# Second layer of a spectral mixture kernel: its seven products a unit in two pairs of runs in place of four

## The chip, the cores and the metric

The kernel runs on one core of one Trainium2 chip. The metric is device time in microseconds, the median of the timed runs. Beside them one execution was recorded by the hardware profiler, and all rows come from it. TensorE (PE) runs the matrix products and its weight loads (PEld), VectorE (DVE) and ScalarE (ACT) the element-wise work, GpSimd (POOL) the scattered stores, SyncE (SP) the other transfers.

## The reference

```python
def _attn_ref(x, filt_r, filt_i):            # x: 8 x 3072 x 256
    Y = np.fft.rfft(x, axis=1) * (filt_r + 1j * filt_i)[None, :, :]
    return np.fft.irfft(Y, n=x.shape[1], axis=1)

def _moe_ref(x, w_gate, w_output_gate, w1, w2):   # one of 8 experts for each token, 256 -> 1024 -> 256
    ...
    h = np.maximum(x[mask] @ w1[e], 0.0)
    out[mask] = gate_w[mask, None] * eom[mask, e, None] * (h @ w2[e])

def _moe2_ref(x, w_in, w_out):               # 256 -> 2048 -> 256, the second layer
    h = np.maximum(x @ w_in, 0.0)
    return h * h @ w_out
```

The three follow one another on 24576 tokens. The change touches the last one alone.

## The kernel before, in words

The kernel works through the filter, the routing and the first (expert) layer, and then through the second layer, which takes a little over half of the span. All sums are made from split numbers: each float32 operand is the sum of a high part and a low part (`bh`, `bl` for tokens, `wsh`, `wsl` and `woh`, `wol` for weights, `hh`, `hl` for the hidden values), and each product is three matrix products into the same PSUM place: high by high, and the two mixed ones.

The second layer has 48 tiles of 512 tokens (t) and in each 8 units of 256 hidden columns (u), 384 units in all. A unit has an up part and a down part.

The up part, `up2`, makes a 2 x 2 block product from seven products in place of eight, on block sums that were made ahead (`split_t` for the tokens, `decode_all` for the weights). The helper `prod` issues one product, three matrix products of 128 x 128 weights with 256 columns. Products 0, 4, 5 and 2 add up in one PSUM bank, V; products 3 and 6 in another, G; product 1 stands in a third, P. The banks are handed over by copies: after product 0 ScalarE copies V to `s1` (L906), after product 3 it copies G to `p5` (L908), after product 4 V to `u2` (L913), after product 2 V to the result block `C[:, 2]` (L921). VectorE makes `C[:, 0]` from P and s1 (L911), `C[:, 3]` from V and p5 (L917), `C[:, 1]` from G and u2 (L918), and then q, the square of the rectified C (L923). V has two buffers, G and P have one each. Where a bank is written again after a copy, the matrix product's weight load waits for that copy.

`split_h` makes the high part `hh` of q on ScalarE (L930) and the low part `hl` on VectorE (L932). `down2` then issues 24 matrix products (m from 0 to 23) into the two output banks of the tile; after the last unit of a tile ScalarE copies the banks out (L951), and GpSimd scatters them to the output rows (L954).

All are Python generators: each `next` issues the instructions up to the next `yield`, and the order in which the loop in `steps_m` takes them is the order of the instructions on every engine. In step n the loop issues the up part of unit n, `split_h` of unit n - 1 and the down part of unit n - 2. Before the change it does so in four parts: 6 up and 3 down matrix products, 6 and 6, 6 and 9, 3 and 6. `hh` stands in the second part, `hl` in the third. Between units `split_t` issues one of its four steps for the next tile, in four of eight units. Below, a run is a row of matrix products of one kind (up or down), and a pair is a run of up and the run of down behind it.

Of the kernel before, what the change touches and what calls it, by code (L numbers as in the profile page):

```python
# [17 lines left out]
ALU = mybir.AluOpType  # L18
# [84 lines left out]
def spectral_moe_kernel(ctx: ExitStack, tc: tile.TileContext, x, filt_r, filt_i, w_gate, w_og, w1, w2,  # L103
                        w_in, w_out, c_ma, c_mi, c_mb, c_mb2, c_sg, c_cum, out):
    nc = tc.nc
# [608 lines left out]
    def py_tiles(t):  # L714
        return [pl["psY2" if t % 2 and "psY2" in pl else "psY"].tile([128, TT], F32, name=f"py{h}") for h in range(2)]
# [82 lines left out]
    def up(t, f):  # L798
        xh, xl = X[t]
        w = width[t]  # L800
        h1, l1 = (a[:, 0] for a in W[t, f // 2])
        f2 = f % 2
        ps = ph_tile()[:, 0:w]
        n = 0
        for c in range(2):
            for a, b in ((h1, xh), (h1, xl), (l1, xh)):
                nc.tensor.matmul(ps, a[:, c, f2 * 128:(f2 + 1) * 128], b[:, c, 0:w], start=n == 0, stop=n == 5)  # L807
                n += 1
        hh = pl["hp"].tile([128, TT], F32R, name="hh")[:, 0:w]
        hl = pl["hp"].tile([128, TT], F32R, name="hl")[:, 0:w]  # L810
        nc.scalar.activation(hh, ps, AF.Relu)  # L811
        tick[:] = [hh[0:1, 0:1].bitcast(F32)]
        nc.vector.scalar_tensor_tensor(hl, ps, 0.0, hh.bitcast(F32), op0=ALU.max, op1=ALU.subtract)  # L813
        H[t, f] = hh, hl
# [77 lines left out]
    def up2(t, u):  # L892

        bh, bl, _ = X2[t]
        wsh, wsl = w2nd[0:2]

        def prod(ps, a, b, start):
            for n, (x, y) in enumerate(((wsh, bh), (wsh, bl), (wsl, bh))):
                nc.tensor.matmul(ps, x[:, u, a], y[:, b], start=start and n == 0, stop=n == 2, skip_group_check=True)  # L899

        bank = lambda name: pl[name].tile([128, TT], F32, name="px" if name == "psX" else "ph")[:, 0:256]
        V, G, P = bank("psH"), bank("psX"), bank("psH2")
        s1, p5, u2 = (pl["sp"].tile([128, 256], F32, name=n) for n in ("s1", "p5", "u2"))
        C = pl["cp"].tile([128, 4, 256], F32, name="C")
        prod(V, 0, 0, True)
        nc.scalar.copy(s1, V)  # L906
        prod(G, 3, 3, True)
        nc.scalar.copy(p5, G)  # L908
        yield
        prod(P, 1, 1, True)  # L910
        nc.vector.tensor_tensor(C[:, 0], P, s1, ALU.add)  # L911
        prod(V, 4, 4, False)
        nc.scalar.copy(u2, V)  # L913
        yield
        prod(G, 6, 2, False)
        prod(V, 5, 5, False)
        nc.vector.tensor_tensor(C[:, 3], V, p5, ALU.add)  # L917
        nc.vector.tensor_tensor(C[:, 1], G, u2, ALU.add)  # L918
        yield
        prod(V, 2, 6, False)  # L920
        nc.scalar.copy(C[:, 2], V)  # L921
        q = pl["cp"].tile([128, 4, 256], F32, name="q")
        nc.vector.scalar_tensor_tensor(q, C, 0.0, C, op0=ALU.max, op1=ALU.mult)  # L923
        H2[t, u] = q
        yield

    def split_h(t, u):
        q = H2[t, u]
        hh, hl = (pl["h2p"].tile([128, 4, 256], F32R, name=n) for n in ("hh2", "hl2"))
        nc.scalar.copy(hh, q)  # L930
        yield
        nc.vector.tensor_tensor(hl, q, hh.bitcast(F32), ALU.subtract)  # L932
        H2[t, u] = hh, hl
        yield

    def down2(t, u):

        hh, hl = H2[t, u]
        woh, wol = w2nd[2:4]
        if u == 0:  # L940
            Z[t] = [p.rearrange("p (c d) -> p c d", c=2) for p in py_tiles(t)]
        for m in range(24):
            k, i, c, n = m // 12, m // 6 % 2, m // 3 % 2, m % 3
            x, w = ((hh, woh), (hl, woh), (hh, wol))[n]
            nc.tensor.matmul(Z[t][k][:, c, :], x[:, 2 * i + k, c * 128:(c + 1) * 128], w[:, 2 * u + i, :],  # L945
                             start=u == 0 and m in (0, 12), stop=u == NU - 1 and m in (11, 23), skip_group_check=True)
            if u == NU - 1 and m in (11, 23):
                if k == 0:
                    Z[t].append(pl["oup"].tile([128, 4, D], F32, name="ou"))
                ou = Z[t][2]  # L950
                nc.scalar.copy(ou[:, 2 * k:2 * k + 2, :], Z[t][k])  # L951
                io = X2[t][2]
                for c in range(2 * k, 2 * k + 2):
                    nc.gpsimd.indirect_dma_start(out=outv[4 * t + c], out_offset=bass.IndirectOffsetOnAxis(ap=io[:, c:c + 1], axis=0),  # L954
                                                 in_=ou[:, c, :], in_offset=None)
            if m in (2, 8, 17):
                yield
        del H2[t, u]
        if u == NU - 1:
            del X2[t], Z[t]  # L960
        yield
# [3 lines left out]
    units2 = [(t, u) for t in range(NTILE2) for u in range(NU)]  # L965
# [3 lines left out]
    def step_1(t, f):  # L969

        last = t + 1 == KP
        if f == 5 and t + 2 == KP:
            start_t(KP)
        if f == 1 and t + 1 >= KP:
            for n in (t + 2, t + 3) if last else (t + 3,):
                if n < NMAIN:
                    start_t(n)
        if f == 1 and last:
            gather(KP)
        if f == 3 and t + 2 < NMAIN and t + 2 != KP:  # L980
            gather(t + 2)
        if f % 2 == 1:

            g = NQ * t + f // 2 + 2
            if NQ * KP <= g < NQ * NMAIN:
                split_w(*divmod(g, NQ))
            if NQ * KP <= g + 2 < NQ * NMAIN:
                load_w(*divmod(g + 2, NQ))
        if t + 1 < NMAIN:
            at = (4, 5, 7) if last else (2, 4, 6)  # L990
            if f == at[0]:
                scale_x(t + 1)
            if f == at[0] + 1:
                put_ids(t + 1)
            if f in at[1:]:
                turn_x(t + 1, at.index(f) - 1)
        elif f == 1:
            load_t(0)
            load_t(1)
        if f not in (1, 5) and dec and next(dec[0], 0) == 0:  # L1000
            dec.clear()
            dcs.close()
            pl["bp0"] = ctx.enter_context(tc.tile_pool(name="bp0", bufs=1))
            pl["bp0"].tile([128, 16], F32, name="pad0")
        if t + 1 == NMAIN and f >= 3:
            if f == 3:
                first.append(split_t(0))
            next(first[0], None)

    def extra(t):  # L1010

        start_t(t)
        gather(t)
        for q in range(3):
            load_w(t, q)
        scale_x(t)
        put_ids(t)
        turn_x(t, 0)
        turn_x(t, 1)
        for f in range(NF + 1):  # L1020
            if f < NF:
                if f % 2 == 0:
                    split_w(t, f // 2)
                    if f == 0:
                        load_w(t, 3)
                up(t, f)
            if f:
                down(t, f - 1)

    def steps_m():  # L1030
        for n in range(len(jobs) + LAG1):
            if n < len(jobs):
                t, f = jobs[n]
                up(t, f)
                step_1(t, f)
            if n >= LAG1:
                down(*jobs[n - LAG1])
            yield
        used = nc.values_load(usedi[0:1, 0:1], min_val=0, max_val=NTILE_T)
        with tc.If(used > NTILE_T - NX):  # L1040
            for t in range(NMAIN, NTILE1):
                extra(t)
        m1.close()
        xgs.close()
        open_m2()
        st = iter(())
        for n in range(len(units2) + 2):
            g = up2(*units2[n]) if n < len(units2) else iter(())
            t, u = units2[min(n, len(units2) - 1)]
            d = down2(*units2[n - 2]) if n >= 2 else iter(())  # L1050
            for part in range(4):
                next(g, None)
                if part == 0 and 0 < n <= len(units2):
                    sh = split_h(*units2[n - 1])
                if part in (1, 2) and n:
                    next(sh, None)
                next(d, None)
            if u == 2 and t + 2 < NTILE2:
                load_t(t + 2)
            if u == 3 and t + 1 < NTILE2:  # L1060
                st = split_t(t + 1)
            next(st, None)
            yield
# [41 lines left out]
    gens = {"a": steps_a(), "b": steps_b(), "c": steps_c()}  # L1105
    done = {"a": 0, "b": 0, "c": 0}
    m = steps_m()
    dec = []
    pre = None
    ready_m = False  # L1110
    close_at = len(order) - 1 - order[::-1].index("b") + 2
    for i, k in enumerate(order):
# [3 lines left out]
        n = done["a"]  # L1116
# [62 lines left out]
```

## Time and profile before

| what | value |
|---|---|
| timed runs, median (lowest to highest) | 3820.49 us (3819.74 to 3821.23) |
| the profiled execution, its own time | 3807.87 us |
| its span | 3806.2 us |
| TensorE busy | 3757.5 us, 99% of the span |
| VectorE busy | 2769.3 us, 73% |
| ScalarE busy | 1980.2 us, 52% |
| granted TensorE clock, mean | 0.998 |

Matrix products overlap in the records: one lasts some 0.28 us, but the next starts after less than half of that. What counts is the time from start to start. The matrix products of the second layer stand at L899 (up) and L945 (down).

### The profile page before, as it was taken

The page shows a single profiled execution, that of the slowest core. Times are in us where ns is not written, and L with a number is a line of the kernel's source. Part 1 is how long each engine was busy: PE and PEld are TensorE (multiplying, and loading weights), DVE is VectorE, ACT ScalarE, POOL GpSimd, SP SyncE. Part 2 cuts the span into 40 slices and gives each one's busy share as a digit, 9 for nine tenths or more (in the row PEclk, how much of TensorE's full clock was granted, in tenths as well). Part 3 has the DMA queues.
Part 4 walks back from the last instruction along what each step waited for, and adds up shares of the span by engine and source line. Part 5 has one row for each costly group of instructions (what it writes and reads, how often), then busy time and mean ns, then how long its engine had stood idle before and what let it go on. Part 6 is the DMA issues. An engine that isn't in the chain of part 4 may idle for free.

```text
span 3806.2 us, 73317 instructions
## 1 busy us (share of the span) xinstructions
PE 3757.5 (99%) x27256; PEld 3510.1 (92%) x27256; DVE 2769.3 (73%) x5041; ACT 1980.2 (52%) x3912; POOL 608.2 (16%) x641
## 2 busy tenths in 40 slices
PE   8999999999999999999999999999999999999998
PEld 7888877888888888888999999999999999999998
DVE  6687685688888865665777777777777777777775
ACT  6476473454554554554555555555555555555554
POOL 3477575000000000000011001000100110011001
PEclk9999999999999999999999999999999999999999
DMA  6333322455555554553000100010000001000100
GB/s 192 100 114 117 107 90 100 153 168 160 172 174 165 173 165 151 162 157 93 23 26 26 29 23 29 23 29 23 29 25 27 24 29 29 24 26 26 29 18 18
DMA packets 262750, 309.29 MB, mean 81 GB/s; under 512 B 75154, under 2 KB 206195, under 8 KB 262387
## 3 DMA queue, kind: packets, MB, share of 16 engines
q1 hardware_dynamic: 242928, 252.39, 21.9%
q0 software_dynamic: 18432, 51.93, 3.8%
q8 instruction: 215, 3.52, 0.4%
q14 instruction: 149, 1.21, 0.1%
q10 hardware_dynamic: 1026, 0.23, 0.0%
HBM read 224.01 MB, written 80.45 MB: 80 GB/s over the span
## 4 chain that ended last, share of the span: by engine, by line
PE 52%; issue 1%; POOL 0%; POOLq 0%; DVE 0%; ACT 0%; DVEq 0%; ACTq 0%
PE py L945 27%; PE ph L899 18%; PE px L899 7%; POOL out_dram L954 0%; POOLq L1174 0%; DVE C L917 0%; ACT u L913 0%; DVEq L917 0%; POOLq L954 0%; ACTq L913 0%
## 5 line engine op out<-in xcount | busy, mean ns | idle before, releaser
L945 PE MATMUL py<-woh,hh 128*128 128x256 f32 x3072 | 857.1, 279 | 0.0
L945 PE MATMUL py<-woh,hl 128*128 128x256 f32 x3072 | 852.8, 278 | 0.5 <-DVE hl L932 0.5
L945 PE MATMUL py<-wol,hh 128*128 128x256 f32 x3072 | 852.9, 278 | 0.0
L954 POOL DMA_INDIRECT out_dram<-ou,ix x192 | 214.0, 1115 | 2924.3 <-ACT ou L951 2880.5
L945 PEld LDWEIGHTS py<-woh,hl 128*128 128x128 f32 x3072 | 579.9, 189 | 1.0 <-DVE hl L932 0.9
L945 PEld LDWEIGHTS py<-woh,hh 128*128 128x128 f32 x3072 | 579.9, 189 | 0.0
L945 PEld LDWEIGHTS py<-wol,hh 128*128 128x128 f32 x3072 | 576.3, 188 | 0.0
L811 ACT ACTIVATE hh<-ph 128x512 fp32r<-128x512 f32 (+1 forms) x472 | 252.2, 534 | 577.4 <-PE ph L807 560.6
L899 PE MATMUL ph<-bh,wsh 128*128 128x256 f32 x1920 | 540.8, 282 | 6.0 <-SPq L1040 4.8
L899 PE MATMUL ph<-bl,wsh 128*128 128x256 f32 x1920 | 537.1, 280 | 0.0
L899 PE MATMUL ph<-bh,wsl 128*128 128x256 f32 x1920 | 536.8, 280 | 0.0
L813 DVE SCALAR_TENSOR_TENSOR hl<-ph,hh 128x512 fp32r<-128x512 f32 (+1 forms) x472 | 286.5, 607 | 254.8 <-ACT hh L811 254.1
L923 DVE SCALAR_TENSOR_TENSOR q<-C 128x1024 f32<-128x1024 f32 x384 | 470.5, 1225 | 1.8 <-ACT C L921 1.8
L932 DVE TENSOR_TENSOR hl<-q,hh 128x1024 fp32r<-128x1024 f32 x384 | 466.8, 1216 | 1.1 <-ACT hh L930 1.1
L917 DVE TENSOR_TENSOR C<-ph,p 128x256 f32<-128x256 f32 x384 | 163.3, 425 | 412.7 <-ACT hh L930 403.1
L921 ACT COPY C<-ph 128x256 f32<-128x256 f32 x384 | 144.1, 375 | 525.2 <-PE ph L899 525.2
L930 ACT CAST hh<-q 128x1024 fp32r<-128x1024 f32 x384 | 403.5, 1051 | 1.3 <-DVE q L923 1.3
L899 PEld LDWEIGHTS ph<-bh,wsh 128*128 128x128 f32 x1920 | 362.4, 189 | 7.2 <-issue 4.9
L899 PEld LDWEIGHTS ph<-bh,wsl 128*128 128x128 f32 x1920 | 360.9, 188 | 0.0
L899 PEld LDWEIGHTS ph<-bl,wsh 128*128 128x128 f32 x1920 | 360.9, 188 | 0.0
L824 PE MATMUL py<-hh,wh 128*128 128x512 f32 (+1 forms) x944 | 341.0, 368 | 0.0
L807 PE MATMUL ph<-xh,wh 128*128 128x512 f32 (+1 forms) x944 | 339.3, 359 | 0.0
(265 smaller groups left out, 8086.7 us busy)
## 6 DMA issues: line engine op xcount, KB each, us to landing
r<-in_moe_w_dram SPq DMA_DIRECT2D x448, 256.0 KB
xt<-in_x_dram SPq DMA_DIRECT2D x48, 512.0 KB
r<-ytd SPq DMA_DIRECT2D x48, 512.0 KB
xg<-srt SPq DMA_DIRECT2D x41, 544.0 KB
ytd<-yt SPq DMA_DIRECT2D x41, 512.0 KB
xg<-srt SPq DMA_DIRECT2D x18, 272.0 KB
ytd<-yt SPq DMA_DIRECT2D x18, 256.0 KB
raw<-in_moe_w_in_dram SPq DMA_DIRECT2D x16, 256.0 KB
```

The costliest lines, as they stand in the source:

```text
L807: nc.tensor.matmul(ps, a[:, c, f2 * 128:(f2 + 1) * 128], b[:, c, 0:w], start=n == 0, stop=n == 5)
L811: nc.scalar.activation(hh, ps, AF.Relu)
L813: nc.vector.scalar_tensor_tensor(hl, ps, 0.0, hh.bitcast(F32), op0=ALU.max, op1=ALU.subtract)
L824: nc.tensor.matmul(Y[t][h], a[:, f % 2, h * 128:(h + 1) * 128], b, start=f == 0 and i == 0, stop=f == NF - 1 and i == 2, skip_group_check= ...
L899: nc.tensor.matmul(ps, x[:, u, a], y[:, b], start=start and n == 0, stop=n == 2, skip_group_check=True)
L917: nc.vector.tensor_tensor(C[:, 3], V, p5, ALU.add)
L921: nc.scalar.copy(C[:, 2], V)
L923: nc.vector.scalar_tensor_tensor(q, C, 0.0, C, op0=ALU.max, op1=ALU.mult)
L930: nc.scalar.copy(hh, q)
L932: nc.vector.tensor_tensor(hl, q, hh.bitcast(F32), ALU.subtract)
L945: nc.tensor.matmul(Z[t][k][:, c, :], x[:, 2 * i + k, c * 128:(c + 1) * 128], w[:, 2 * u + i, :], start=u == 0 and m in (0, 12), stop=u == ...
L954: nc.gpsimd.indirect_dma_start(out=outv[4 * t + c], out_offset=bass.IndirectOffsetOnAxis(ap=io[:, c:c + 1], axis=0), in_=ou[:, c, :], in_o ...
```

## The change

The seven products of a unit keep their operands, banks and copies. What changes is where the generators yield and in which order the loop takes them. Product 2 of a unit, with its copy and the square, is issued in the next step, behind product 0 of the next unit (`next(old, None)`). From the fourth step on, a step issues 18 up (product 0, product 2 of the unit before, products 3, 1, 4, 6), then `hh`, then 15 down, then `hl`, then 3 up (product 5), then 9 down. In the first step that has a down part (n = 2) the 18 and 15 are parted into 9 and 6 and again 9 and 9. The sum `C[:, 1]` is made ahead of `C[:, 3]`.

```diff
@@ up2
         prod(V, 0, 0, True)
         nc.scalar.copy(s1, V)
+        yield
         prod(G, 3, 3, True)
         nc.scalar.copy(p5, G)
         yield
@@ up2
         prod(V, 4, 4, False)
         nc.scalar.copy(u2, V)
-        yield
         prod(G, 6, 2, False)
+        nc.vector.tensor_tensor(C[:, 1], G, u2, ALU.add)
+        yield
         prod(V, 5, 5, False)
         nc.vector.tensor_tensor(C[:, 3], V, p5, ALU.add)
-        nc.vector.tensor_tensor(C[:, 1], G, u2, ALU.add)
         yield
@@ down2
-            if m in (2, 8, 17):
+            if m in (5, 14):
                 yield
@@ steps_m
+        none = iter(())
+        old = none
         for n in range(len(units2) + 2):
-            g = up2(*units2[n]) if n < len(units2) else iter(())
+            g = up2(*units2[n]) if n < len(units2) else none
             t, u = units2[min(n, len(units2) - 1)]
-            d = down2(*units2[n - 2]) if n >= 2 else iter(())
-            for part in range(4):
-                next(g, None)
-                if part == 0 and 0 < n <= len(units2):
-                    sh = split_h(*units2[n - 1])
-                if part in (1, 2) and n:
-                    next(sh, None)
+            d = down2(*units2[n - 2]) if n >= 2 else none
+            next(g, None)
+            next(old, None)
+            sh = split_h(*units2[n - 1]) if 0 < n <= len(units2) else none
+            next(g, None)
+            if n == 2:
                 next(d, None)
+            next(g, None)
+            next(sh, None)
+            if n > 2:
+                next(d, None)
+            next(d, None)
+            next(sh, None)
+            next(g, None)
+            next(d, None)
+            old = g
```

## Rows read from the trace of the kernel before

**Rows 1.** The page, engines: busy us (share of the span) xinstructions.

```profile
PE 3757.5 (99%) x27256; PEld 3510.1 (92%) x27256; DVE 2769.3 (73%) x5041; ACT 1980.2 (52%) x3912; POOL 608.2 (16%) x641
```

**Rows 2.** Windows: 500 us, then the four pairs of one unit; columns as headed.

```profile
core 0: us, PE busy (x) PEld busy (x) DVE busy (x) ACT busy (x) POOL busy (x), PEclk, DMA share, GB/s
2250.00:2750.00 500.00, 500.00 (x4290) 500.00 (x4290) 369.68 (x574) 260.26 (x547) 50.62 (x46) 1.00 0.09 26
...
2603.23:2604.30 1.07, 1.07 (x12) 1.07 (x11) 1.07 (x2) 1.07 (x3) 0.00 (x0) 1.00 0.72 172
2604.30:2605.67 1.37, 1.37 (x15) 1.37 (x13) 0.56 (x2) 0.80 (x4) 0.00 (x0) 1.00 0.00 0
2605.67:2607.44 1.77, 1.77 (x17) 1.77 (x16) 0.79 (x3) 0.89 (x1) 0.00 (x0) 1.00 0.00 0
2607.44:2608.47 1.03, 1.03 (x11) 1.03 (x10) 1.03 (x2) 0.38 (x1) 0.00 (x0) 1.00 0.00 0
```

**Rows 3.** Timeline of TensorE, same unit: start us, length us, engine, line, operation.

```profile
2604.65 0.28 PE L899 MATMUL ph<-bh,wsh 128*128 128x256 f32 x1
...
2605.67 0.28 PE L899 MATMUL px<-bh,wsh 128*128 128x256 f32 x1
...
2606.50 0.28 PE L945 MATMUL py<-woh,hl 128*128 128x256 f32 x1
...
2607.44 0.28 PE L899 MATMUL ph<-bh,wsh 128*128 128x256 f32 x1
```

**Rows 4.** Timeline, same unit: ScalarE's operations and G's last product of product 3.

```profile
2605.51 1.05 ACT L930 CAST hh<-q 128x1024 fp32r<-128x1024 f32 x1
...
2608.05 0.38 ACT L921 COPY C<-ph 128x256 f32<-128x256 f32 x1 [1.49 <-PE ph L899]
...
2609.07 0.28 PE L899 MATMUL px<-bh,wsl 128*128 128x256 f32 x1
...
2609.44 0.38 ACT L908 COPY p<-px 128x256 f32<-128x256 f32 x1
```

**Rows 5.** Timeline of VectorE, same unit.

```profile
2606.65 0.42 DVE L917 TENSOR_TENSOR C<-ph,p 128x256 f32<-128x256 f32 x1 [1.31 <-ACT hh L930]
...
2606.99 0.41 DVE L918 TENSOR_TENSOR C<-px,u 128x256 f32<-128x256 f32 x1
...
2607.32 1.22 DVE L932 TENSOR_TENSOR hl<-q,hh 128x1024 fp32r<-128x1024 f32 x1
...
2608.46 1.23 DVE L923 SCALAR_TENSOR_TENSOR q<-C 128x1024 f32<-128x1024 f32 x1
```

**Rows 6.** Timeline, the second unit, ahead of all down products (PEld: weight loads).

```profile
1780.77 0.28 PE L899 MATMUL ph<-bh,wsl 128*128 128x256 f32 x1
...
1781.08 0.38 ACT L906 COPY s<-ph 128x256 f32<-128x256 f32 x1
...
1781.45 0.28 PE L899 MATMUL ph<-bh,wsl 128*128 128x256 f32 x1
...
1781.51 0.19 PEld L899 LDWEIGHTS ph<-bh,wsh 128*128 128x128 f32 x1
...
1781.73 0.28 PE L899 MATMUL ph<-bl,wsh 128*128 128x256 f32 x1
...
1782.20 0.28 PE L899 MATMUL px<-bh,wsl 128*128 128x256 f32 x1
```

**Rows 7.** Timeline, a unit in which a weight load was held once.

```profile
3220.91 0.42 DVE L917 TENSOR_TENSOR C<-ph,p 128x256 f32<-128x256 f32 x1 [1.66 <-ACT hh L930]
...
3221.24 0.28 PE L945 MATMUL py<-wol,hh 128*128 128x256 f32 x1
...
3221.39 0.19 PEld L899 LDWEIGHTS ph<-bh,wsh 128*128 128x128 f32 x1
...
3221.62 0.29 PE L899 MATMUL ph<-bl,wsh 128*128 128x256 f32 x1
...
3221.97 0.28 PE L945 MATMUL py<-woh,hl 128*128 128x256 f32 x1
```

More of the change, by code (lines that the diff above doesn't have):

```diff
@@ L913, in up2 @@
         nc.scalar.copy(u2, V)
+        prod(G, 6, 2, False)
+        nc.vector.tensor_tensor(C[:, 1], G, u2, ALU.add)
         yield
-        prod(G, 6, 2, False)
         prod(V, 5, 5, False)
         nc.vector.tensor_tensor(C[:, 3], V, p5, ALU.add)
-        nc.vector.tensor_tensor(C[:, 1], G, u2, ALU.add)
         yield
```

## The prediction

> **What bounds the kernel now.** I read the page first: the TensorE line is at 99% of the span, the next engine at 73% [rows 1]. Such a share could hide waits, so I went to the windows. In the second layer TensorE starts 4290 products in 500 us at a granted clock of 1.00, the upper of its two levels [rows 2]; that is 116.55 ns from start to start, and 45 products, one unit, take 5.245 us. No wait of TensorE on another engine is left in it. So the time is 384 units at the pitch of the product stream, and only two things can move it: the pitch, or a new wait.
>
> The reader is to see next that the pitch isn't one number. The four pairs of runs of one unit (6 up + 3 down, 6 + 6, 6 + 9, 3 + 6) take 1.07, 1.37, 1.77 and 1.03 us [rows 2]: 119, 114, 118 and 114 ns a product (the program's 9, 12, 15 and 9 products; the view counts also those that reach over an edge). Inside a pair it settles: nine pitches from 2604.65 to 2605.67 give 113.3 ns, eight from 2606.50 to 2607.44 give 117.5 ns [rows 3]. Up and down products stand in both kinds of pair, so it isn't the product; the pitch changes where the stream goes from down back to up, every other pair slow. I call them the fast and the slow pitch, 113.5 and 117.5 ns. What each pair has beyond product count times pitch is its entry: 1.37 - 12 x 0.1135 = 0.01 us for a fast pair, 1.77 - 15 x 0.1175 = 0.01 us for a slow one.
>
> **The change part by part.** No product, copy or DMA is added or removed. Three things move.
>
> *Fewer pairs.* Two pairs a unit, 33 and 12 products. With alternation kept, one of them is fast and one slow. Large pair fast: 33 x 0.1135 + 12 x 0.1175 + 2 x 0.01 = 5.176 us, 0.07 under 5.245. Large pair slow: 33 x 0.1175 + 12 x 0.1135 + 0.02 = 5.260 us, 0.015 over. The extra parting in the first full unit (9 + 6, 9 + 9, 3 + 9) makes three pairs there, which selects the first of the two if nothing else resets the alternation. In itself it costs one entry, 0.01 us, once.
>
> *Product 3 and product 6 of the bank G come together.* G is written by product 3, copied by ScalarE (p5, L908), and written again by product 6, which must wait for the copy. Before, 15 products lie between the two; after, the order is product 0, the old unit's product 2, product 3, products 1 and 4, product 6: six products lie between. Is that long enough? From the start of G's last product to the start of the copy: 2609.07 to 2609.44, 0.37 us; the copy 0.38 us [rows 4]. From the end of a releasing operation to the held weight load: 3220.91 + 0.42 = 3221.33 to 3221.39, 0.06 us [rows 7]; from ScalarE 1781.08 + 0.38 = 1781.46 to 1781.51, 0.05 us [rows 6]. Together 0.37 + 0.38 + 0.05 = 0.80 us. The waiting instruction is the weight load, which goes out when the product ahead of its own starts, so it is due six pitches after G's last product: 6 x 0.1135 = 0.68 us at the fast pitch, 0.705 at the slow one. It is late by 0.12 or 0.095 us, in every unit.
>
> That such a lateness is paid in full, two places show. In the unit before the first down products the same distance occurs, between product 0 and product 4 of bank V: weight load due at 1781.45, out at 1781.51, the product two on at 1781.73, where two pitches after 1781.45 would be 1781.68 [rows 6]: 0.05 us lost with a copy that had started 0.31 us after its product instead of 0.37. At 3221.24 a late VectorE sum held a weight load to 3221.39, and 0.23 us passed from there to the second product [rows 7], two pitches: the delay is lost once, with no further price of a restart. Behind the held load every later product of the unit queues, 15 down products of another unit included; nothing can pass.
>
> The Trainium skill, Perfetto Trace Analysis, section Optimizing Tensor Performance (Matmuls), asks that groups rotate through different PSUM banks, so that the evacuation of one overlaps the products of the next. It speaks against this change: V and G are each written again inside one unit, and G's return is brought nearer. The held load of rows 6 agrees; by that rule and by the rows the sum is the same.
>
> *What the restart does to the pitch.* A pause can reset the alternation. After 1781.51 four pitches take 1781.73 to 1782.20, 117.5 ns, slow, although the stream ahead of it was fast (1780.77 to 1781.45, six pitches, 113 ns); after 3221.39 it stays slow (3221.62 to 3221.97, three pitches, 117 ns) in a pair that was fast until then [rows 6, 7]. So the parity chosen by the first full unit's extra parting doesn't survive the pause. If the stream goes on slow from product 6 through the 15 down products, the large pair is slow nearly throughout: 5.26 + 0.095 = 5.355 us. If it falls back to fast: 5.176 + 0.12 = 5.296 us. Lower bound of the pause: the 0.31 us start of rows 6, 0.31 + 0.38 + 0.05 - 0.68 = 0.06, or 5.236 us with the fast pitch. I take the middle of the first two, 5.33 us, since both restarts shown go slow but only their first products can be followed; both ends stay in the range.
>
> *Product 2 moves into the next unit, behind its product 0.* It now follows the sum C3 (L917) that VectorE does behind the residual hl (L932). That closes a loop from one unit to the next: product 2 to copy 0.37, copy 0.38, to square q 0.03, q 1.23, to cast hh about 0.05, hh 1.05, to hl 0.03, hl's place on VectorE 1.14 (2607.32 to 2608.46), C3 0.42, to the load 0.06, and three pitches 0.35 [rows 4, 5, 7]. The sum is 5.11 us, of which the two gaps around hh are estimates from the gap of 0.03 between the copy and q. The unit of 5.33 us leaves 0.2 us, so I cost it at nothing. Its cover is that 0.2 us alone. In four of eight units the split of the next tile (up to four subtractions at 0.34 us each, the pitch of 2606.65 to 2606.99 [rows 5], 1.36 us) stands between C3 and q; VectorE is free there from C3's start + 0.34 until q, which waits for three pitches, 0.37, 0.38 and so on: about 1.45 us, so it just fits. The down products use hh and hl of two units back, ready 2 us ahead, so the larger runs don't make them late.
>
> Start and end: at the start product 2 of the first units is covered by three more products, but waits for C3 behind hl; at the end the last square comes 0.7 us later against the last 24 products. I put 1 us on it, with bounds of 0 and 3.
>
> **Sum.** Units with down products: 382. (5.33 - 5.245) x 382 = 32 us, plus 1: 33 us. The profiled execution took 3807.87 us (span 3806.2, 1.7 around it), so 3841 us in its terms. The three timed runs have a median of 3820.49, 12.6 us above it; I let the difference stand, since nothing in the trace assigns it, and add the 33 us to the median: 3853 us. The case's own range: 5.296 gives 19 + 0 us, 3840; 5.355 gives 42 + 3 us, 3865.
>
> **Rivals.** A change under 0.2%, 7.6 us, can't be told from none here.
>
> 1. Product 6 doesn't pause and the large pair is fast: (5.176 - 5.245) x 382 = -26 us, 3794 us. For it: the pairs of rows 2 are regular, and the extra parting fits the alternation. Against it: the copy chain would have to be under 0.68 us, where its parts add to 0.80. It decides as soon as the chain takes less than 6 pitches. Chance 0.11.
>
> 2. The pause is there but about pays for itself: 0.06 us and a fast large pair, (5.236 - 5.245) x 382 = -3 us, or 0.12 us with almost all pairs fast (45 x 0.1135 + 0.02 + 0.12 = 5.25, +1 us): 3817 to 3822 us. For it: copies that start 0.31 us after their product exist [rows 6]. The Trainium skill, Perfetto Trace Analysis, section Identifying Dependency Chains, says that instructions that wait on several engines may have a separate semaphore instruction ahead of them, which would fit a later start once buffers come round again; no row here shows that instruction. Against it: in the steady unit the start is 0.37 us [rows 4]. Chance 0.10.
>
> 3. The loop through VectorE binds as well: each 0.1 us by which its gaps are longer than taken, beyond the 0.2 us, costs 38 us. With 0.3 us, 5.43 us a unit: 3820 + 71 = 3891 us. For it: 5.11 us of a loop with eight hand-overs. Against it: five of these gaps are measured. Chance 0.07.
>
> The forecast keeps 0.72.
>
> **How the numbers follow.** Predicted: 3853 us, the likeliest case. Range: its own 3840 to 3865, widened to case 2 below and some for the end and the pitch above, 3814 to 3870; left out are case 1 and case 3, together 0.18. Faster by over 0.2%: case 1, 0.11. Within 0.2%: case 2, 0.10. Slower: 0.72 + 0.07 = 0.79.
>
> **What would show it.** In the changed kernel's timeline the weight load of product 6 (px, L899) should start about 0.05 us behind the end of p5, some 0.1 us later than the product ahead of it, once a unit; 500 us should hold about 4220 products (45 x 500 / 5.33) instead of 4290; the pitch of the 15 down products tells slow from fast. I am wrong in the pause if that load starts with the product ahead of it; wrong in the pitch if the run of 15 is at 113.5 ns throughout; wrong in the loop if product 2's load starts 0.05 us behind C3's end.

## The result, and the profile after

The changed kernel takes 3861.59 us (median of four executions, 3855.9 to 3861.97) beside 3820.86 us of the kernel before on the same chip: ratio 1.0105, 95% interval 1.0089 to 1.012, 40.7 us slower. The forecast was 3853 us and a range of 3814 to 3870.

The page of the changed kernel, its span and the engine line:

```profile
span 3854.2 us, 72841 instructions
...
PE 3796.2 (98%) x27256; PEld 3538.4 (92%) x27256; DVE 2782.3 (72%) x5041; ACT 2025.5 (53%) x3912; POOL 607.9 (16%) x641
```

TensorE still shows 98% where it had 99% [rows 1]: the share hides the loss. The windows show it. The same 500 us, late in the second layer:

```profile
2250.00:2750.00 500.00, 500.00 (x4222) 497.68 (x4221) 365.77 (x560) 267.47 (x540) 53.59 (x48) 1.00 0.09 25
```

4222 products where there were 4290 [rows 2], at the same clock of 1.00: 118.4 ns from start to start, 5.329 us a unit. The forecast said about 4220, and 5.33 us.

First and last product of the second layer, from the timeline (its length is the difference):

```profile
1788.28 0.55 PE L899 MATMUL ph<-bh,wsh 128*128 128x256 f32 x1 [4.95 <-SPq L1041]
...
3843.38 0.28 PE L946 MATMUL py<-wol,hh 128*128 128x256 f32 x1
```

3843.38 - 1788.28 = 2055.1 us. In the profiled execution of before the layer runs from 1775.50 to 3795.36, 2019.9 us. So the second layer is 35.2 us longer, of which the forecast had 33. The profiled spans differ by more, 48 us, since the second layer starts 12.8 us later; the code ahead of it is the same. The kernels below tell where that comes from: those that ran beside a before of 3807 us start the layer at 1773 to 1777 us, those beside a before of 3819 to 3821 us (the changed kernel is one) at 1786 to 1788 us. In the traces it arises at two places of the code ahead, near 560 and near 600 us, where TensorE stands still for some microseconds and the granted clock falls: 0.89 in the window of 550 to 560 us and 0.66 in that of 600 to 610, where before has 1.00 in both. All five kernels that start the layer late, and no other, have these two falls. So it most likely goes with the chip, and is most likely the 12.6 us between the profiled execution of before and its timed runs that the prediction left unassigned; why TensorE stops there stays open. All lengths below are of the second layer, so this shift is in none of them.

The place of the pause, in the timeline of one unit (the last product of product 3, the copy p5, the last product of product 4, the held load of product 6, and products behind it):

```profile
2604.61 0.28 PE L899 MATMUL px<-bh,wsl 128*128 128x256 f32 x1
...
2604.98 0.37 ACT L909 COPY p<-px 128x256 f32<-128x256 f32 x1
...
2605.32 0.28 PE L899 MATMUL ph<-bh,wsl 128*128 128x256 f32 x1
...
2605.41 0.19 PEld L899 LDWEIGHTS px<-bh,wsh 128*128 128x128 f32 x1
...
2605.63 0.28 PE L899 MATMUL px<-bl,wsh 128*128 128x256 f32 x1
...
2605.97 0.28 PE L946 MATMUL py<-woh,hl 128*128 128x256 f32 x1
...
2607.45 0.28 PE L946 MATMUL py<-wol,hh 128*128 128x256 f32 x1
```

The copy starts 0.37 us after the product and ends at 2604.98 + 0.37 = 2605.35; the load goes out at 2605.41, 0.06 us behind it. It was due with the product ahead, at 2605.32: held by 0.09 us. The down products of this unit then run fast: from the second, at 2605.97, to the last of the 15, at 2607.45, are 13 pitches of 113.8 ns; the six pitches ahead of the pause (2604.61 to 2605.32) are of 118 ns. The start-to-start time at this place, over 380 units, has a mean of 206 ns against 117 around it: 0.089 us a unit, 34 us in all.

No view of waits names it. The list of TensorE's waits for this stretch is empty, and the groups of weight loads have one row with more than 1 us of idle time ahead of it, without a releaser:

```profile
L899 PEld LDWEIGHTS px<-bh,wsh 128*128 128x128 f32 x713 | 134.3, 188 | 8.1
```

The 713 are the first loads of products 3 and 6 together, so some 356 of them are held. The row has 8.1 us of idle time for them, where the start-to-start times give 356 x 0.089 = 32 us: a held load overlaps the product ahead, whose record ends 0.28 us after its start, and most of the pause stands as busy time.

### The profile page after: what moved, and what is told of

Same layout as the page of the kernel before. It is cut to its first block, busy times and chain, and to the rows that moved or that the text cites. A ratio compares the mean times of both kernels' runs of the same rounds, so it can differ in the third digit from the quotient of the medians.

```text
span 3854.2 us, 72841 instructions
## 1 busy us (share of the span) xinstructions
PE 3796.2 (98%) x27256; PEld 3538.4 (92%) x27256; DVE 2782.3 (72%) x5041; ACT 2025.5 (53%) x3912; POOL 607.9 (16%) x641
## 4 chain that ended last, share of the span: by engine, by line
PE 50%; issue 3%; POOL 0%; DVE 0%; ACT 0%; POOLq 0%
PE py L946 26%; PE ph L899 17%; PE px L899 7%; POOL out_dram L955 0%; DVE q L924 0%; DVE hl L933 0%; ACT hh L931 0%; POOLq L1185 0%; ACT C L922 0%; ACT p L909 0%; ACT ou L952 0%; DVE C L919 0%; ACT s L906 0%; POOLq L955 0%
## 5 line engine op out<-in xcount | busy, mean ns | idle before, releaser
L906 ACT COPY s<-ph 128x256 f32<-128x256 f32 x384 | 143.6, 374 | 673.1 <-PE ph L899 673.1
L807 PE MATMUL ph<-xl,wh 128*128 128x512 f32 (+1 forms) x944 | 338.1, 358 | 0.7 <-DVE xl L792 0.7
```

## The experiments

Each kernel ran beside the kernel before; "shorter" and "longer" below are groups of executions of one kernel. Where a unit's time or a length is given without a row, it is from start to start of matrix products in that kernel's trace.

**1. The near place taken away.** Product 3 goes ahead of the old unit's product 2, so nine products lie between products 3 and 6.

```diff
             next(g, None)
+            next(g, None)
             next(old, None)
             sh = split_h(*units2[n - 1]) if 0 < n <= len(units2) else none
-            next(g, None)
             if n == 2:
```

> The changed kernel with product 3 put ahead of the old unit's product 2, so that nine products lie between product 3 and product 6 instead of six; all else as in the change. Theory A (the load of product 6 waits for the copy p5): nine pitches are 1.02 us against the 0.80 us of the chain, the pause goes, and with the alternation set by the extra parting the large pair is fast: 5.18 us a unit, the second layer some 1993 to 1998 us long against 2055 in the changed kernel and 2020 before; if the alternation falls the other way, 5.26 us and 2025. The loop through VectorE has 0.07 us left then and may hold product 2 in some units. Theory B (longer runs make the stream slow, the copy is beside the point): the second layer stays at about 2055 us.

Measured: 3815.97 us beside 3807.35 us, ratio 0.9987 (0.9956 to 1.0018), but in two groups: six executions of ten at 3816 to 3822 us, four at 3781 to 3783. The profiled one is a longer one. Windows, 500 us and then three pairs near the start of the layer (9 + 9, 3 + 9, the first 18 + 15):

```profile
2250.00:2750.00 500.00, 500.00 (x4275) 500.00 (x4274) 369.76 (x572) 269.55 (x546) 53.05 (x46) 1.00 0.09 26
1785.93:1788.05 2.12, 2.12 (x20) 2.12 (x19) 1.79 (x3) 1.16 (x2) 0.00 (x0) 1.00 0.00 0
1788.05:1789.43 1.38, 1.38 (x15) 1.38 (x13) 1.19 (x2) 0.16 (x1) 0.00 (x0) 1.00 0.00 0
1789.43:1793.32 3.89, 3.89 (x35) 3.89 (x34) 2.26 (x5) 2.36 (x5) 0.00 (x0) 1.00 0.02 4
```

No load is held in the steady stretch; the unit is 5.267 us in every one, the length 2029.2 us, 25.9 us under the changed kernel. So theory A holds for the pause, and B falls: the runs are as long as in the changed kernel and the pause is gone. But in this execution the pitch came out the other way: 33 products in 3.89 us, 118 ns, are slow, and 12 in 1.38 us, 115 ns with the entry, fast. The forecast of 5.26 us and 2025 us for that case was right in size.

**2. The same without the extra parting.**

```diff
-            if n == 2:
-                next(d, None)
             next(g, None)
             next(sh, None)
-            if n > 2:
-                next(d, None)
+            next(d, None)
             next(d, None)
```

> As the run with product 3 ahead, but without the extra parting of the first full unit. Theory A with alternation carried from pair to pair: the large pair is now the slow one, 5.26 us a unit, the second layer about 2025 us, some 30 us over the run with the parting. Rival (the pitch does not depend on the parity of pairs): within 3 us of the run with the parting.

Measured: 3782.21 us (four executions, 3780.17 to 3784.81), ratio 0.9934 (0.9917 to 0.9951). Windows, 500 us and then the end of the first large pair (15 down), the 3 + 9 and the next 18 + 15:

```profile
2250.00:2750.00 500.00, 500.00 (x4351) 500.00 (x4351) 376.40 (x583) 273.07 (x558) 54.17 (x48) 1.00 0.09 27
1788.77:1790.54 1.77, 1.77 (x18) 1.77 (x17) 1.44 (x3) 1.24 (x2) 0.00 (x0) 1.00 0.00 0
1790.54:1791.95 1.41, 1.41 (x14) 1.41 (x13) 1.29 (x2) 0.09 (x1) 0.00 (x0) 1.00 0.00 0
1791.95:1795.71 3.76, 3.76 (x36) 3.76 (x34) 2.16 (x4) 2.23 (x5) 0.00 (x0) 1.00 0.02 4
```

4351 products; the unit is 5.174 us and the length 1994.3 us, where the sum of the prediction for a fast large pair was 5.176 us. The size of the two forms is confirmed; which of them comes was forecast the wrong way round. In both kernels the alternation begins one pair later than the forecast counted. After the pauses at the start of the layer the stream comes back slow (9 + 9 in 2.12 us, 118 ns; 15 in 1.77 us, 118 ns), and the first change from down to up leaves it slow: in the first kernel 6 down ahead of the 9 + 9 were slow too (1785.23 to 1785.93, 117 ns), in the second the 3 + 9 behind take 1.41 us, 117.5 ns. Only the following ones alternate. This is no rule, though. In three other traces (the second series below, and the kernels with the parting in experiments 6 and 7) the stream comes back slow as well, and the first change makes it fast: in the first kernel with parting of experiment 6, 6 down at 117 ns and the 9 up behind them at 115, in the second series 3 + 9 at 114 ns behind down products at 118. What decides at the first change stays open.

A second series of this kernel on another chip:

> The kernel with product 3 ahead of product 2 and no parting once more, on another chip: theory, the large pair fast in all or nearly all executions (5.17 us a unit, 1994 us of second layer) and 25 us under before; if the start leaves either form at random, some executions lie about 36 us over the others.

Measured: 3782.68 us median beside 3807.66, ratio 0.9964 (0.9933 to 0.9995), again two groups: four executions at 3779 to 3783 us, two at 3816 to 3818, 35 us over them. The profiled one is a longer one, 2030.2 us of layer; in it the granted clock is at its lower level as late as the first down run, and the first full 18 up behind are slow (windows; the clock is the 1.00 or 0.50 near the end):

```profile
1785.87:1787.00 1.13, 1.13 (x7) 1.13 (x7) 0.77 (x3) 1.03 (x2) 0.00 (x0) 0.50 0.00 0
1789.55:1791.67 2.12, 2.12 (x20) 2.12 (x19) 0.40 (x1) 1.17 (x4) 0.00 (x0) 1.00 0.00 0
```

18 products in 2.12 us, 118 ns. So by their times the large pair came out fast in eight of ten executions without the parting and in four of ten with it. The same program comes out in either form, so the form is set as an execution runs; each of the three profiled executions has its form from the first unit of 18 + 15 on. That the parting shifts the odds is not shown by these counts alone; experiment 7 has more.

**3. The changed kernel without the parting** (the diff of experiment 2 on the changed kernel).

> The changed kernel without the extra parting of the first full unit, and nothing else. Theory A (the pause at product 6 resets the alternation in every unit): the second layer within 3 us of the changed kernel's 2055 us, its large runs slow as there. Rival (the parting sets which pair is slow, pause or not): 25 to 32 us away from it.

Measured: 3838.07 us beside 3807.35, ratio 1.0081 (1.0064 to 1.0098); the length is 2053.6 us, 1.5 us under the changed kernel.

```profile
2250.00:2750.00 500.00, 500.00 (x4224) 498.01 (x4223) 365.04 (x565) 268.94 (x542) 53.42 (x48) 1.00 0.09 27
```

4224 products against 4222. In the profiled executions the parting does nothing once the pause is in every unit, as theory A said. The medians leave more open: this kernel lies 30.7 us over its before, the changed kernel 40.7 over its own, since the profiled execution here is the longest of four (3843.25 us) and there the shortest (3855.9 us).

**4. The near place put into the kernel before.**

```diff
         prod(V, 0, 0, True)
         nc.scalar.copy(s1, V)
-        prod(G, 3, 3, True)
-        nc.scalar.copy(p5, G)
-        yield
         prod(P, 1, 1, True)
         nc.vector.tensor_tensor(C[:, 0], P, s1, ALU.add)
+        yield
         prod(V, 4, 4, False)
         nc.scalar.copy(u2, V)
+        prod(G, 3, 3, True)
+        nc.scalar.copy(p5, G)
         yield
```

> The kernel before with its four pairs of runs as they were, but products 0 and 1 in the first and 4 and 3 in the second up run, so that only the six down products lie between product 3 and product 6. Theory A: a pause of 0.10 to 0.12 us a unit in the old form of the pairs, the second layer 35 to 48 us over the 2020 us of before. Theory B (the loss comes with the long runs): within 3 us of before.

Measured: 3900.31 us beside 3807.35, ratio 1.0246 (1.0229 to 1.0263); length 2111.7 us, 92 us over before, about twice the forecast.

```profile
2250.00:2750.00 500.00, 499.79 (x4110) 490.42 (x4109) 347.97 (x547) 251.21 (x523) 49.24 (x44) 1.00 0.08 24
```

The edit had a second near place that the expectation missed: with product 1 in the first run, products 0 and 4 of bank V also stand six apart. The start-to-start times show both: 55 us at product 4, 35 us at product 6. Theory B is out, but the price of one place had to be measured cleanly:

```diff
-            if m in (2, 8, 17):
+            if m in (2, 5, 17):
```

with products 0 and 1 in the first up run and 3 and 4 in the second.

> The kernel before with its four pairs, products 0 and 1 in the first up run, 3 and 4 in the second, and the down runs cut 3, 3, 12, 6 instead of 3, 6, 9, 6, so that six products lie between 3 and 6 and nine between 0 and 4: one near place only. Theory A: one pause of 0.09 to 0.12 us a unit, the second layer 33 to 48 us over the 2020 us of before, about half of what the kernel with two near places lost. Theory B: within 5 us of before.

Measured: 3855.05 us beside 3819.28, ratio 1.0092 (1.0077 to 1.0108); length 2055.1 us, 35.2 us over before. The timeline of one unit, from the last product of product 3 to the load of product 6:

```profile
2604.60 0.28 PE L899 MATMUL px<-bh,wsl 128*128 128x256 f32 x1
...
2604.97 0.37 ACT L911 COPY p<-px 128x256 f32<-128x256 f32 x1 [0.66 <-PE px L899]
...
2605.32 0.28 PE L945 MATMUL py<-wol,hh 128*128 128x256 f32 x1
...
2605.40 0.19 PEld L899 LDWEIGHTS px<-bh,wsh 128*128 128x128 f32 x1
```

Copy 0.37 us after the product, load at 2605.40 where 2605.32 was due: 0.08 us held, now with down products in between, in four pairs (6 + 3, 6 + 3, 6 + 12, 3 + 6). Its unit is 0.091 us longer than that of before, and the step at the held load has 0.089 of it over the pitch around: the whole loss of the change is had by this one nearness alone.

**5. Nearer still.** In the changed kernel products 1 and 3 are exchanged; three products lie between.

```diff
-        prod(G, 3, 3, True)
-        nc.scalar.copy(p5, G)
-        yield
         prod(P, 1, 1, True)
         nc.vector.tensor_tensor(C[:, 0], P, s1, ALU.add)
+        prod(G, 3, 3, True)
+        nc.scalar.copy(p5, G)
+        yield
         prod(V, 4, 4, False)
```

> The changed kernel with products 1 and 3 exchanged, so that three products lie between product 3 and product 6 instead of six; products 0 and 4 stay nine apart. Theory A (the copy chain of 0.80 us is paid above the pitches that cover it): the pause grows by three pitches, from 0.09 to 0.44 us a unit, and the second layer from 2055 to some 2165 to 2200 us. Theory B (the 0.09 us is a fixed cost of any held load): about 2055 us.

Measured: one execution, 3963.92 us beside 3819.28; length 2164.8 us. Here the pause is long enough for the view of waits:

```profile
PEld px L899 <- ACT p L911: 119.0, 319, 0.4
```
```profile
2250.00:2750.00 500.00, 484.30 (x4006) 466.80 (x4005) 347.38 (x533) 252.12 (x512) 50.25 (x46) 1.00 0.09 25
```

By the start-to-start times, the two steps at the held load take 0.44 us a unit more than two pitches, as forecast: 0.35 us over the 0.09 us of six products, three pitches. The pause is what the chain of 0.80 us has left over the pitches that cover it, not a fixed price. The length grew by 110 us rather than 0.35 x 382 = 134, because after these longer pauses the stream comes back at the fast pitch in 379 of 380 units, and the unit is the fast form plus the pause: 5.174 + 0.446 = 5.620 us.

**6. A small pair as small as can be.** Experiment 2 with the runs 18 + 21 and 3 + 3.

```diff
-            if m in (5, 14):
+            if m in (5, 20):
```

> Product 3 ahead of the old unit's product 2, no extra parting, and the runs cut at 18 up with 21 down and 3 up with 3 down, so that only six products of a unit stand in the second pair. Theory (two alternating pitches, one entry a pair): 39 x 0.1133 + 6 x 0.1175 + 0.03 = 5.155 us a unit where the large pair is fast, the second layer about 7 us shorter than the 1994 us of the 18 with 15 form; where it falls the other way, 5.285 us and 2036. Rival (the slow pitch belongs to a place in the unit, product 5 and what follows it, or to a time of about 1.4 us): the slow stretch stays twelve products long and the length stays 1994 us. The loop through VectorE may hold product 2, since product 5 comes 0.7 us later.

Measured: 3838.91 us beside 3819.28, ratio 1.0052 (1.0038 to 1.0066); length 2038.7 us. It starts in the form hoped for, 5.147 us in its first units (forecast 5.155), and leaves it in the seventh. There, in the timeline (C3, q and hh of the step before, hl, C3, the products ahead, the held load of product 2, products behind):

```profile
1812.90 0.42 DVE L919 TENSOR_TENSOR C<-ph,p 128x256 f32<-128x256 f32 x1
...
1814.69 1.22 DVE L924 SCALAR_TENSOR_TENSOR q<-C 128x1024 f32<-128x1024 f32 x1
...
1815.94 1.05 ACT L931 CAST hh<-q 128x1024 fp32r<-128x1024 f32 x1 [0.74 <-DVE q L924]
...
1817.03 1.23 DVE L933 TENSOR_TENSOR hl<-q,hh 128x1024 fp32r<-128x1024 f32 x1 [0.45 <-ACT hh L931]
...
1818.17 0.42 DVE L919 TENSOR_TENSOR C<-ph,p 128x256 f32<-128x256 f32 x1
...
1818.47 0.28 PE L899 MATMUL px<-bl,wsh 128*128 128x256 f32 x1
...
1818.59 0.28 PE L899 MATMUL px<-bh,wsl 128*128 128x256 f32 x1
...
1818.64 0.19 PEld L899 LDWEIGHTS ph<-bh,wsh 128*128 128x128 f32 x1
...
1818.86 0.28 PE L899 MATMUL ph<-bl,wsh 128*128 128x256 f32 x1
...
1819.10 0.28 PE L899 MATMUL ph<-bh,wsh 128*128 128x256 f32 x1
```

C3 ends at 1818.17 + 0.42 = 1818.59, the load follows at 1818.64, and was due with the product at 1818.59: 0.05 us. This is the loop through VectorE of the prediction, in a unit behind the step of four subtractions, which here take 1.46 us (1813.23 to 1814.69) where the prediction had 1.36. From C3 to C3 are 1.79 us to q, 1.25 to hh, 1.09 to hl and 1.14 to C3, 5.27 us against a unit of 5.147. After it the pitch is slow (1818.86 to 1819.10, 120 ns), the unit 5.293 us, which leaves the loop room; nothing is held again, and the slow form stays for the rest.

```profile
2250.00:2750.00 500.00, 500.00 (x4253) 500.00 (x4252) 367.71 (x569) 269.14 (x543) 55.64 (x48) 1.00 0.09 27
```

With the parting:

> The same with the extra parting of the first full unit. Theory: the parting moves the alternation by one pair, and the first pair after the long pause at the start does not change the pitch; so the large pair is slow in most executions, about 2036 us of second layer, some 45 us over the run without the parting. Rival (which pair is slow has nothing to do with the parting): the same as the run without it.

Measured: 3837.09 us, ratio 1.005 (1.0034 to 1.0065), length 2036.4 us. Not the other form: it too starts fast, keeps it through two holds of this kind, eight units apart, and loses it at the third, 16 units later than the run without. The expectation missed; the hold, not the parting, ends the fast form here. Since two holds of the same length (0.05 us) left it alone, a hold can end it but need not.

**7. The loop cut.** hl is issued behind product 5 and C3.

```diff
             next(d, None)
-            next(sh, None)
             next(g, None)
+            next(sh, None)
             next(d, None)
             old = g
```

> As the run with 18 up and 21 down, 3 up and 3 down (product 3 ahead of product 2, no parting), and hl of the unit before issued behind product 5 and its sum C3 instead of ahead of them, so that C3 no longer waits for hl and the loop through VectorE is cut. Theory (that run lost its fast form because once a tile product 2's load was held by 0.05 us behind hl and C3): no load is held in the steady stretch, and whichever form the start leaves stays; 5.15 us a unit and a second layer of some 1985 us if the large pair comes out fast, 5.29 and 2037 if slow. Rival (the short small pair can't hold the fast form by itself): it falls to 5.29 us within some units without any held load.

Measured: 3769.03 us beside 3807.66, ratio 0.9899 (0.9885 to 0.9913); one of the four executions took 3825.32. Profiled: length 1981.5 us, 5.147 us in every unit of the steady stretch, no load held. So the small pair can hold the fast form by itself, and the rival of the expectation falls.

```profile
2250.00:2750.00 500.00, 500.00 (x4374) 500.00 (x4373) 376.02 (x587) 271.06 (x558) 53.84 (x48) 1.00 0.09 28
```

4374 products. The expectation for a fast large pair was 1985 us. Repeated:

> The run with 18 up and 21 down, 3 up and 3 down, hl behind C3, no parting, once more: theory, the start leaves either form at random and it then stays, so the executions fall in two groups some 55 us apart, the faster one about 38 us under before; the share of each tells how far the start decides. Rival (the one slow execution of the first run was chance): all executions in the faster group.

Measured: 3769.45 us beside 3808.05, ratio 0.99 (0.9884 to 0.9917), all four executions at 3769 to 3771 us. Seven of eight in the shorter group: 38.6 us under the before of the same chip, where the changed kernel lay 40.7 us over its own, so both are beaten unless the start throws it. The longer execution has the same granted clock as the others, 0.998, and its 57 us fit the slow large pair (2038.7 us of layer in experiment 6, 1981.5 here); it was not profiled. With the parting:

> The same with the extra parting of the first full unit, which moves the alternation by one pair: theory, the other of the two forms than the run without the parting, 1985 against 2037 us, provided that the start leaves the same pitch in both; no held load in the steady stretch in either.

Measured: one execution of four at 3767.53 us, the profiled one, with the same 5.147 us a unit; three at 3824 to 3826, median 3824.8. Seven of eight executions in the shorter group without the parting and one of four with it, together with experiments 1 and 2 fifteen of eighteen against five of fourteen: the parting seems to favour the longer form, the theory's direction, though not in every execution, and the traces don't show by what.

## Why the prediction was right, point by point

**The pause.** Right in place, chain and size. The chain measured 0.37 + 0.37 + 0.06 = 0.80 us, the forecast; held 0.08 us where the products ahead are slow and 0.11 where they are fast, forecast 0.095 and 0.12. Shown by taking it away (experiment 1: no load held, 25.9 us of length back although the large pair was slow in all units), by putting it alone into the old order (experiment 4: +35.2 us) and by lengthening it (experiment 5). The Trainium skill, Perfetto Trace Analysis, section Optimizing Tensor Performance (Matmuls), asks for groups that rotate through PSUM banks; these runs agree, with 0.09 us for a bank that comes back after six products and none after nine.

**The two forms of the pairs.** Right in size: 5.176 and 5.260 us forecast, 5.174 and 5.267 measured without the pause (experiments 1 and 2).

**The pitch after the restart.** I took the middle between always slow and back to fast, 5.33 us, and the mean over the layer came out so; that part was luck, since it comes from kinds of units that I didn't have. Over 380 units of the changed kernel the median pitch of the 15 down products is slow (over 116 ns) in 267 and fast (under 114.5 ns) in 113. In 127 units the up products ahead of the pause are fast, and behind it the down products are then slow, without exception; in 113 units up is slow and down fast. Both kinds take 5.313 us at the median. In 140 units both are slow, 5.347 us at the median, near my upper end of 5.355. A large pair that is fast on both sides of the pause, my lower end of 5.296, doesn't occur. Here the pause changes a fast stream to slow every time; what decides after a slow one stays open.

**The parity of the extra parting.** Wrong: that it "selects the first of the two if nothing else resets the alternation". By the times of experiments 1, 2 and 7 the other form comes more often with it, and only by odds. In two traces the first change behind the restart at the start of the layer keeps the pitch, in three it doesn't, so the step that failed is the count of pairs from a known start: the start is not the same in every execution. In the profiled executions of the changed kernel with and without it (experiment 3) it did not matter, as the prediction said.

**The loop through VectorE at nothing.** Nearly right. In the unit shown above, hl, C3 and the load of product 2 stand as follows:

```profile
2607.38 1.23 DVE L933 TENSOR_TENSOR hl<-q,hh 128x1024 fp32r<-128x1024 f32 x1 [0.46 <-ACT hh L931]
...
2608.52 0.42 DVE L919 TENSOR_TENSOR C<-ph,p 128x256 f32<-128x256 f32 x1
...
2609.22 0.19 PEld L899 LDWEIGHTS ph<-bh,wsh 128*128 128x128 f32 x1
```

C3 ends at 2608.52 + 0.42 = 2608.94, 0.28 us ahead of the load; less the hand-over of 0.05 us that is 0.23, where the forecast had 0.2. In 31 units, all of one place in the eight, the load of product 2 was held, 2.7 us in all. One of them (hl, a scatter of GpSimd, C3, the held load):

```profile
2015.29 1.27 DVE L933 TENSOR_TENSOR hl<-q,hh 128x1024 fp32r<-128x1024 f32 x1 [0.46 <-ACT hh L931]
2015.31 0.96 POOL L955 DMA_INDIRECT out_dram<-ou,ix  x1 [0.30 <-issue]
...
2016.80 0.42 DVE L919 TENSOR_TENSOR C<-ph,p 128x256 f32<-128x256 f32 x1 [0.24 <-PE ph L899]
...
2017.28 0.19 PEld L899 LDWEIGHTS ph<-bh,wsh 128*128 128x128 f32 x1
```

This isn't the loop growing longer, for hl starts no later than in other units, 1.59 to 1.63 us ahead of product 0. It runs beside the last scatter of a tile, lasts 1.27 us where it otherwise lasts 1.23, and C3 starts 1.51 us behind its start where it otherwise starts at 1.14. The product named as C3's releaser had ended 0.8 us earlier (2015.98, product 5), so C3 waited for something else. Of the 47 units with such a scatter beside hl, C3 is late by 0.28 us or more in 30 and by 0.06 in 17; what makes the difference stays open. The remaining one of the 31 is the first full unit of the layer. In a shorter unit the loop did bind (experiment 6).

**Start and end, and the rest.** 1 us was forecast, with bounds of 0 and 3. Counted by products, the changed kernel is 1.1 us behind after the first 84 of the layer and loses another 0.8 us over the last 50, some 1.9 us; at the start the granted clock also stays at its lower level for longer, 6.8 against 3.4 us, so not all of that is the order's. The 33.4 us between are 33.8 of pauses and 2.7 of holds, less some 3 us that the mixed pitch gives back. Of the 40.7 us between the medians the profiled layer has 35.2. The profiled execution took 3855.9 us, 35.0 over the median of before; the other three are 6 us longer. A larger share of slow units would do that, but those three were not profiled, so it stays open.

**The rivals.** Case 1 needed a chain under 0.68 us: it was 0.80. Case 2 needed 0.06 us, or fast pairs nearly throughout: neither came. The early copy start of 0.31 us that spoke for it belongs to the start of the layer: the trace of before has a 17 ns semaphore instruction of ScalarE ahead of 382 of the 384 copies of L908, which start 0.37 us or more behind their product, and none ahead of the five copies of the layer that start at 0.31 to 0.32; the prediction saw no such instruction in its rows. Of case 3 came the 2.7 us above, and not by longer hand-overs.

## What to carry to other kernels

Where one engine runs without a gap, price a new order by the distance between the write of a bank and its rewrite: copy start, copy, hand-over, against the pitches from the bank's last product to its rewrite, less one because the weight load goes out with the product ahead: as many pitches as there are products in between. At 0.80 us to six products of 0.1135 us a tenth of a microsecond was lost in each of 382 units, and three products more in between cost nothing and gave it back. And a gain that rests on a self-repeating state of a stream, as the fast large pair here, has to be free of any other hold, however small: in experiment 6 one of 0.05 us ended it for the rest of the layer.

## What the runs showed of the hardware that was not expected

The pitch of matrix products of 256 columns, at one granted clock of 1.00, has two values, 113.3 and 117.5 ns, that alternate from pair to pair of up and down runs for whole layers, unit after unit to the nanosecond: 5.174 or 5.267 us for the same program in different executions, 35 us of layer. Of four holds of 0.05 us two flipped it and two left it alone (experiment 6). A pause of 0.44 us was followed by the fast pitch 379 times of 380, one of 0.08 to 0.11 us in 113 units of 380 in the changed kernel, and there never where the stream ahead was fast. A wait of 0.09 us doesn't show in the lists of waits, and hardly in TensorE's busy share, 98% against 99%.
